# The product with w_out by one level of Strassen's method, in a fused spectral-mixing and squared-ReLU kernel

## The chip, the cores and the metric

The kernel runs on one core of one Trainium2 chip. Times are device microseconds (us) of one execution, and lower is better. Most executions of one kernel agree within 0.3%. An execution that is more than 1.5% above the fastest of the same kernel is called slow and is left out of every comparison.

Engine names are as in the profile: PE is TensorE's matmuls, PEld its weight loads, DVE is VectorE, ACT is ScalarE, POOL is GpSimd.

## The reference

```python
x: (8, 3008, 256) float32;  w_in: (256, 2048) float64;  w_out: (2048, 256) float64
X = fft(fft(x, axis=1), axis=2).real.astype(float32)     # 8 sequences of 3008 rows
h = X.reshape(24064, 256) @ w_in
g = maximum(h, 0) ** 2
out = (g @ w_out).astype(float32)
```

## The kernel before

The transform over the 256 columns is applied to w_in once. The transform over the 3008 rows is made of matrix products, after each sequence's rows have been *folded*: rows that share a table entry are added and subtracted on VectorE. A sequence has six folds and twelve groups of *transform products*. They are made for the next sequence while the main products of the present one run.

The main work is cut into blocks of 256 columns, and a block into 16 *units*, one for each 128 columns of w_in. A unit has a front (two products, then VectorE's combination, then relu and square on ScalarE) and a back (the products with w_out).

```python
def fold(b, t):                                   # six for each sequence
    tt(out=s, in0=v[0::2], in1=v[1::2], op=add)            # fs  } VectorE, two inputs in SBUF each
    tt(out=d, in0=v[0::2], in1=v[1::2], op=subtract)       # fd  }
    # ... load of the next rows ...
    nc.scalar.copy(sc[..., 0:H+1:H], s[..., 0:H+1:H])      # four elements for each partition
    tt(out=sc[..., 1:H], ...); tt(out=dc, ...)
    for kp in range(2):
        tt(out=wP[r, kp], ...); tt(out=wQ[r, kp], ...)
    # ... wE: a copy of one column of wP to all, on ScalarE ...

def front(b, k0, n, fc):
    nc.tensor.matmul(hP, G1[:, fs], pt[:, ks]); nc.tensor.matmul(hQ, G2[:, fs], qt[:, ks])
    nc.vector.scalar_tensor_tensor(out=t, in0=et, scalar=gE[:, fc:fc+1], in1=hP, op0=mult, op1=add)
    tt(out=g[:, 0:n], in0=t, in1=hQ, op=add)               # row k
    tt(out=g[:, n:...][:, ::-1], in0=t, in1=hQ, op=subtract)   # row S - k
    act(g, g, Relu); act(g, g, Square)

def back(b, k0, n, fc, g):
    # for both sides, for each 128 columns of g:
    nc.tensor.matmul(po[s][0:m, j], g[:, ...], wout[:, fc], ...)   # g is the stationary operand
    # after the last fc: copy to SBUF on ScalarE, store

# for each unit: front; back of three units earlier; a share of the next sequence's folds and
# transform products, spread evenly over the sequence
```

A fold's VectorE instructions have both inputs in SBUF, the front's have one in SBUF and one in PSUM, and GpSimd does no arithmetic.

## Time and profile before

The first three executions had a median of 2299.17 us.

| | busy, share of the span | what it does |
|---|---|---|
| TensorE | 96% | two products in the front and four in the back of each unit |
| VectorE | 51% | front, folds, rounding of the float64 weights at the start |
| ScalarE | 46% | relu, square, copies |
| GpSimd | 1% | starts loads, no arithmetic |

This is the groups-of-instructions view of the kernel before, with different shapes kept apart. After the bar come busy us in total and the mean ns of one, then the idle time before it and what ended that.

```profile
L194 DVE TENSOR_TENSOR wP<-sc 128x129 f32<-128x129 f32 x64 | 18.4, 288 | 0.0
L188 DVE TENSOR_TENSOR sc<-fs 128x254 f32<-128x254 f32 x32 | 13.6, 425 | 15.3 <-ACT sc L187 15.3
L189 DVE TENSOR_TENSOR dc<-fd 128x254 f32<-128x254 f32 x32 | 13.4, 417 | 0.0
```

These are the undisturbed lengths: 0.29, 0.43 and 0.42 us. The middle line shows that VectorE waits 15.3/32 = 0.48 us on average for ScalarE's copy of four elements.

### The profile page before, as it was taken

The numbers are of one execution on the slowest core, as the hardware profiler recorded it, in microseconds if no ns is written. First come the engines' busy times: TensorE is split into PE (matmuls) and PEld (weight loads), VectorE is DVE, ScalarE is ACT, GpSimd is POOL, SyncE is SP. The second block draws the span as 40 slices with busy tenths as digits, with TensorE's granted clock in tenths as the row PEclk, the third lists the DMA queues.
The fourth block names the chain that finished last, engine by engine and source line by source line (L and its number), as shares of the span: only waits on it lengthen the run. The fifth ranks groups of instructions, "written<-read, shape, count | busy, mean of one in ns | idle before, by whom it ended". The sixth has DMA issues, their size and how long they took to land.

```text
span 2298.1 us, 26257 instructions
## 1 busy us (share of the span) xinstructions
PE 2213.2 (96%) x9888; PEld 1865.0 (81%) x9888; DVE 1182.4 (51%) x2932; ACT 1049.4 (46%) x1809; POOL 28.1 (1%) x56
## 2 busy tenths in 40 slices
PE   3679999999999999999999999999999999999998
PEld 1357888888888888888888888888888888888887
DVE  5597444654446544474445644465444644444443
ACT  0124444554445444454445544455444544445554
POOL 0000000000000000000000000000000000000000
PEclk7789999999999999999999999999999999999999
DMA  6221000110001000010000100010000000000000
GB/s 212 72 74 45 19 10 10 36 46 10 10 10 54 28 10 10 28 54 10 19 10 27 55 10 10 10 52 30 10 10 18 10 10 10 19 9 10 19 10 18
DMA packets 38528, 64.29 MB, mean 28 GB/s; under 512 B 3448, under 2 KB 27768, under 8 KB 37888
## 3 DMA queue, kind: packets, MB, share of 16 engines
q1 hardware_dynamic: 30096, 33.04, 4.5%
q0 software_dynamic: 7488, 29.31, 4.2%
q8 instruction: 77, 1.26, 0.2%
q14 instruction: 51, 0.42, 0.1%
q10 hardware_dynamic: 816, 0.26, 0.1%
HBM read 37.96 MB, written 24.64 MB: 27 GB/s over the span
## 4 chain that ended last, share of the span: by engine, by line
PE 94%; DVE 5%; ACT 0%; DMA 0%; issue 0%; ACTq 0%; DVEq 0%
PE po L275 57%; PE ph L252 14%; PE ph L251 14%; PE pd L217 8%; PE pg L157 1%; DVE fs L129 0%; DVE fd L134 0%; DVE fs L135 0%; DVE fs L143 0%; DVE fd L133 0%; DVE fs L141 0%; PE pe L162 0%; DVE fs L127 0%; DVE win L144 0%; DVE fd L139 0%; DVE wout L144 0%
## 5 line engine op out<-in xcount | busy, mean ns | idle before, releaser
L275 PE MATMUL po<-wout,g 128*128 128x256 f32 (+1 forms) x6144 | 1460.2, 380 | 1.1 <-ACT g L262 1.1
L275 PEld LDWEIGHTS po<-wout,g 128*128 128x128 f32 (+1 forms) x6144 | 1150.2, 188 | 177.9 <-ACT os L282 6.1
L261 ACT ACTIVATE g<-g 128x512 f32<-128x512 f32 (+2 forms) x768 | 476.2, 620 | 1010.8 <-DVE g L259 983.0
L254 DVE SCALAR_TENSOR_TENSOR he<-Et,gE,ph 128x256 f32<-128x256 f32 (+1 forms) x768 | 364.2, 474 | 859.8 <-PE ph L252 859.2
L262 ACT ACTIVATE g<-g 128x512 f32<-128x512 f32 (+2 forms) x768 | 477.1, 621 | 24.4
L251 PE MATMUL ph<-Pt,G 128*128 128x256 f32 (+1 forms) x1536 | 453.6, 377 | 19.5 <-DVE g L259 19.5
L252 PE MATMUL ph<-Qt,G 127*128 127x256 f32 (+1 forms) x1536 | 453.5, 376 | 0.0
L251 PEld LDWEIGHTS ph<-Pt,G 128*128 128x128 f32 x1536 | 292.8, 191 | 82.3 <-DVE g L259 22.8
L258 DVE TENSOR_TENSOR g<-he,ph 128x256 f32<-128x256 f32 (+1 forms) x768 | 319.5, 416 | 67.3 <-DVE he L254 4.1
L252 PEld LDWEIGHTS ph<-Qt,G 127*128 127x128 f32 x1536 | 294.5, 192 | 33.5
L259 DVE TENSOR_TENSOR g<-he,ph 128x256 f32<-128x256 f32 (+2 forms) x768 | 314.2, 409 | 0.0
L217 PE MATMUL pd<-cosT,wP 128*128 128x377 f32 (+3 forms) x192 | 70.7, 502 | 8.4 <-DVE wP L194 6.0
L217 PE MATMUL pd<-sinT,wQ 128*127 128x377 f32 (+3 forms) x192 | 67.5, 490 | 0.0
L217 PE MATMUL pd<-cosT,wE 128*128 128x377 f32 (+3 forms) x192 | 65.7, 479 | 0.0
L217 PEld LDWEIGHTS pd<-cosT,wP 128*128 128x128 f32 (+1 forms) x192 | 37.0, 197 | 30.7 <-DVE wP L194 8.8
L157 PE MATMUL pg<-win,cosd 128*128 128x512 f32 x16 | 14.9, 1083 | 47.4 <-DVE win L144 47.4
L217 PEld LDWEIGHTS pd<-sinT,wQ 128*127 128x127 f32 (+1 forms) x192 | 37.3, 194 | 20.1 <-issue 1.5
L217 PEld LDWEIGHTS pd<-cosT,wE 128*128 128x128 f32 (+1 forms) x192 | 36.5, 190 | 19.1
L196 ACT COPY wE<-wP 128x256 f32<-128x256 f32 (+2 forms) x48 | 19.4, 403 | 70.0 <-DVE wP L194 70.0
L224 ACT COPY da<-pd 128x377 f32<-128x377 f32 (+3 forms) x48 | 22.7, 473 | 57.3 <-PE pd L217 57.3
L157 PEld LDWEIGHTS pg<-win,cosd 128*128 128x128 f32 x16 | 4.7, 324 | 51.8 <-DVE win L144 26.2
L91 POOL DMA_DIRECT2D xt<-in_x_dram x48 | 25.6, 536 | 1537.8 <-DVE fd L182 1537.0
(38 smaller groups left out, 396.0 us busy)
## 6 DMA issues: line engine op xcount, KB each, us to landing
out_dram<-os SPq DMA_DIRECT2D x72, 256.0 KB
xt<-in_x_dram POOLq DMA_DIRECT2D x32, 512.0 KB, 3.8
raw<-in_moe_w_in_dram SPq DMA_DIRECT2D x8, 512.0 KB
raw<-in_moe_w_out_dram SPq DMA_DIRECT2D x8, 512.0 KB
xt<-in_x_dram POOLq DMA_DIRECT2D x8, 484.0 KB, 4.5
xt<-in_x_dram POOLq DMA_DIRECT2D x8, 480.0 KB, 4.5
out_dram<-os SPq DMA_DIRECT2D x24, 128.0 KB
cosT<-in_cos_s_dram POOLq DMA_DIRECT2D x2, 1131.0 KB, 18.4
```

Of the source, the lines that this page charges most:

```text
L91: nc.gpsimd.dma_start(out=xt[b, t][0:rows], in_=x[b, r0:r0 + rows])
L157: nc.tensor.matmul(ps[0:n], tab[:, i], w[:, i], start=i == 0, stop=i == 1)
L217: nc.tensor.matmul(ps, folded[b, t][which][0:rows, kp, 0:n], tab[0:rows, kp, t, 0:nk], start=i == 0, stop=i == 2)
L224: nc.scalar.copy(st["a"], ps)
L251: nc.tensor.matmul(hP, G1[:, fs], pt[:, ks], start=True, stop=True)
L252: nc.tensor.matmul(hQ, G2[:, fs], qt[:, ks], start=True, stop=True)
L254: nc.vector.scalar_tensor_tensor(out=t, in0=et[:, ks], scalar=gE[:, fc:fc + 1], in1=hP, op0=ALU.mult, op1=ALU.add)
L258: tt(out=g[:, 0:n], in0=t, in1=hQ, op=ALU.add)
L259: tt(out=g[:, n:n + hi - lo][:, ::-1], in0=t[:, lo:hi], in1=hQ[:, lo:hi], op=ALU.subtract)
L261: act(g, g, AF.Relu)
L262: act(g, g, AF.Square)
L275: nc.tensor.matmul(po[s][0:m, j], g[:, g0 + o:g0 + o + m], wout[:, fc], start=fc == 0 and j == 0, stop=fc == NFC - 1, skip_group_check=True)
```

## The change

The intent is to make TensorE's work less. One level of Strassen's method turns a 2 by 2 block product of eight products into one of seven. The price is sums of the operands before and of the results after. The sums of w_out's blocks are made once, those of g in every step, and both go to GpSimd, which was idle. The results now come out transposed, so eight small transposes on TensorE turn each block back. Blocks have 251 columns and six of them cover 1505 rows. A *step* now covers two of the former units.

```diff
+    def combine(n, g):                       # every step, GpSimd
+        gt(out=s1, in0=g21, in1=g22, op=ALU.add)
+        gt(out=s2, in0=s1, in1=g11, op=ALU.subtract)
+        gt(out=s3, in0=g11, in1=g21, op=ALU.subtract)
+        gt(out=s4, in0=g12, in1=s2, op=ALU.subtract)
     def back(n, j, g, s):
-                nc.tensor.matmul(po[s][0:m, j], g[:, ...], wout[:, fc], ...)      # 8 for two units
+        for nm, i, w, v in (("mA", 0, wout[:, 0, j, 0:H], g[:, 0, 0]),             # 7 for a step
+                            ("mA", 1, wout[:, 1, j, 0:H], g[:, 1, 0]),
+                            ("mB", 0, wsum[:, 2, j], g[:, 1, 1]),
+                            ("mB", 1, wout[:, 0, j, H:D], s[:, 0]),
+                            ("mC", 0, wsum[:, 0, j], s[:, 1]),
+                            ("mC", 1, wsum[:, 1, j], s[:, 2]),
+                            ("mD", 0, wout[:, 1, j, H:D], s[:, 3])):
+            nc.tensor.matmul(acc[nm][:, i, 0:n], w, v[:, 0:n], ...)
+    def gather(n):                           # end of a block
+        # mA, mB to SBUF on ScalarE; u2, u3, u4 on VectorE; four sums to c on GpSimd
+    def store(b, k0, n, c):
+        # eight nc.tensor.transpose of c, a copy on ScalarE, store
@@ schedule
-    # folds and transform products of the next sequence spread evenly over its units
+            if b + 1 < B:
+                if at < 9 and at % 3:        # at = step within the sequence, 0 to 47
+                    fold(b + 1, at // 3 * 2 + at % 3 - 1)
+                if at == 10:
+                    dft = dft_ops(b + 1)
+        if at >= 10 and at % NJ == 2:        # NJ = 8 steps for a block
+            for f in dft[:5]:
+                f()
+            dft = dft[5:]
```

Cut: smaller pools, loads of x by another queue, sums of w_out, no wE. The schedule is part of the change. The six folds now stand in the first nine steps of a sequence, and the transform products come five operations at a time.

## The prediction

> **What bounds the kernel now.** I read the page first, engine totals and the chain that ended last:
>
> ```profile
> PE 2213.2 (96%) x9888; PEld 1865.0 (81%) x9888; DVE 1182.4 (51%) x2932; ACT 1049.4 (46%) x1809; POOL 28.1 (1%) x56
> ...
> PE 94%; DVE 5%; ACT 0%; DMA 0%; issue 0%; ACTq 0%; DVEq 0%
> PE po L275 57%; PE ph L252 14%; PE ph L251 14%; PE pd L217 8%; PE pg L157 1%; DVE fs L129 0%; DVE fd L134 0%; DVE fs L135 0%; DVE fs L143 0%; DVE fd L133 0%; DVE fs L141 0%; PE pe L162 0%; DVE fs L127 0%; DVE win L144 0%; DVE fd L139 0%; DVE wout L144 0%
> ```
>
> The chain is TensorE for 94% of the span, 57% of it the product with w_out (po), which the change attacks. VectorE and ScalarE are half idle, GpSimd has nothing to do. Next, whether TensorE has gaps, from busy time by stretches:
>
> ```profile
> 115.00:200.00 85.00, 64.36 (x241) 50.64 (x240) 76.39 (x172) 28.16 (x53) 2.13 (x4) 0.88 0.21 67
> 200.00:2282.00 2082.00, 2082.00 (x9448) 1776.44 (x9447) 1043.46 (x2624) 1005.43 (x1723) 17.03 (x32) 1.00 0.07 20
> ```
>
> The columns after the length are busy us (and instructions) of PE, weight loads, DVE, ACT, POOL, then clock. From 200 us on TensorE is never idle at full clock. Busy is not peak, so I took the rate from the timeline, one unit of a 225-column block:
>
> ```profile
> 402.00 1.89 PE L275 MATMUL po<-wout,g 128*128 128x256 f32 x8
> 402.20 0.45 DVE L254 SCALAR_TENSOR_TENSOR he<-Et,gE,ph 128x225 f32<-128x225 f32 x1 [1.25 <-PE ph L252]
> 402.75 0.39 DVE L258 TENSOR_TENSOR g<-he,ph 128x225 f32<-128x225 f32 x1
> 403.06 0.38 DVE L259 TENSOR_TENSOR g<-he,ph 128x224 f32<-128x224 f32 x1
> ...
> 403.72 0.54 PE L251 MATMUL ph<-Pt,G 128*128 128x225 f32 x2
> 404.10 0.55 PE L252 MATMUL ph<-Qt,G 127*128 127x225 f32 x2
> ...
> 404.49 0.38 PE L275 MATMUL po<-wout,g 128*128 128x256 f32 x1
> ```
>
> Units repeat after 404.49 - 402.00 = 2.49 us for 12 matmul instructions (each product shows as two). In blocks of 256 columns the same view repeats after 2.59 us (131.90 to 134.49), so a 256-column instruction takes 0.216 us and a column about 0.83 ns of it. TensorE streams at its rate and a saved column is a saved time.
>
> **What the Trainium skill says.** "TensorE: Matmul & The Clock Gate", Back-to-back issue gap, gives N/2.4 + 2.5 ns for warm matmuls; "FP8 and Floating Point Precision", TensorE Precision Notes, says true FP32 takes four passes. The trace agrees with both: two instructions of two passes each would be 2 x 256/2.4 + 2.5 = 215.8 ns (estimate from the pages), and 0.216 us is measured. "GPSIMD Engine Reference", Elementwise — side-by-side cycle accounting, gives about 2.6 cycles per element at 1.2 GHz for a two-input FP32 operation. No run yet shows this, since the kernel before has no arithmetic on GpSimd. "SBUF — State Buffer", Who interferes with whom, says that a VectorE instruction with two SBUF inputs and a GpSimd instruction that reads SBUF lock each other out. Not seen here either, for the same reason.
>
> **The change part by part.** *Arithmetic of TensorE, before:* 640 units of 2.59 us and 128 of 2.49 us make 1976 us. The transform products are 96 groups of three, 1.90 us each in the chain in order of time: 182 us. The rest of the span, 2298 - 1976 - 182 = 140 us, is the prologue (main work starts at 115 us, of which 12 groups x 1.9 = 23 us are in the 182, so 92), the stage to about 200 us in which w_out is rounded on VectorE beside the first units (about 39), and the tail (9).
>
> *After:* one step covers two units: four front products and seven for eight, each of 251 columns. An instruction is 215.8 - 5 x 0.83 = 211.7 ns, a step 22 x 211.7 = 4.66 us (4.64 in the block of 250). 8 sequences x 8 steps x 6 blocks give 320 x 4.66 + 64 x 4.64 = 1788 us: 188 us less. Two sources: one product in twelve goes (some 165 us), and w_out's product no longer pads 1505 and 1503 rows to 24 tiles of 128 rows (3072 for 3008).
>
> *Transposes back:* 48 blocks x 8 transposes, each 128 x 126 in and out. The closest row of before is the products of one column, which are limited by weight loads:
>
> ```profile
> 75.76 1.75 PEld L162 LDWEIGHTS pe<-altd,win 128*128 128x128 f32 x15 [0.24 <-issue]
> ```
>
> 15 loads in 1.75 us, 0.117 us each. If a transpose needs one load and one pass (the build marks it as a transpose, so I choose that) a block costs 8 x 0.12 = 1.0 us, 48 us in all; as an ordinary FP32 product of two loads it would be near 95 us.
>
> *VectorE:* the front work is the same (three instructions per half), 1.17 us per half (122.96 - 121.79 at the first units), so 2.34 of 4.66 us. Per block come three sums, about 1.2 us. *ScalarE:* relu and square over 1004 elements; from 579 ns for 449 and 629 ns for 512 elements I get 0.8 ns per element and 1.03 us each, 384 x 2 x 1.03 = 790 us for 953 us before. Copies of two accumulators add 1.2 us per block, the copies for wE go (19 us). Neither bounds. *GpSimd:* 2.6 cycles x 251 / 1.2 GHz = 0.54 us, with start about 0.65 us (estimate from the page): four per step are 2.6 of 4.66 us, 1728 of them 1.12 ms. It has room.
>
> *Latency.* A step's w_out products come two steps after its front, 9.3 us. VectorE ends about 1.5 us after the front, ScalarE at 3.7, GpSimd at 6.4. About three to five us of slack, so steady steps should run without a gap. At a block's end the accumulators have one set of banks: ScalarE copies end 4.3 and 4.9 us after the front, the sums at 5.5; the next block's products want those banks from 4.7 to 7.2 us in the same order, so they just fit. The recombined block c ends at 3.75 + 8 x 0.65 = 9.0 us and its transposes are due at 9.3: tight. I put 15 us for these and for bursts of transform products that wait for ScalarE.
>
> *Fold steps.* This is the largest loss. A fold is 2.68 us of VectorE (80.40 - 77.72 in the timeline), all but nothing of it with two SBUF inputs, now in two steps of every three. In such a step VectorE has 2.34 + 2.68 us; its third instruction waits for a small ScalarE copy (before: 0.46 us on average), which now stands behind relu and square, 2.1 us after the front instead of 0.2: another 1.1 us. That is 6.2 us against 4.66. The six instructions that follow coincide with the four GpSimd sums, and if they lock each other out the step takes up to 8.8 us. Over eight steps with six folds, less 2.5 us that VectorE may lag (two PSUM buffers), that loses 3 to 17 us per sequence, six sequences outside the load stage: 20 to 100 us. I put 35, since the fold's placing looks tuned.
>
> *Load stage.* Rounding 5.15 us + front 2.34 + five folds among eight steps, DMA behind them, GpSimd also forming sums of w_out: about 92 us for 37 us of TensorE work, 55 lost for 39 before. *Tail:* copies, sums, GpSimd, transposes, copy, store: 16 us for 9.
>
> *Sum:* 1788 + 182 + 48 + 92 + 55 + 16 + 35 + 15 = 2231, say 2230 us, 3.0% less.
>
> **The rivals.** (1) VectorE and GpSimd lock each other out in full during folds and in the load stage: +70 to +90 us, about 2310, no gain. For it: the page and the coincidence in time; against: VectorE's lag has room, and only 10 of 26 VectorE instructions in such a step have two SBUF inputs. (2) GpSimd is slower than the estimate. At about 1.05 us per instruction its 36 per block reach the block's 37.3 us plus transposes and it becomes the bound; at 1.2 us the time is 1728 x 1.2 + 200 = 2270 or more, and c comes late at each block. Nothing in the profile of before speaks to it. (3) Transposes as two-pass products: +45 us, 2275. (4) All waits hidden: 1788 + 182 + 48 + 92 + 45 + 14 = 2170.
>
> **Range and chances.** The rivals that lose are one-sided and partly exclusive; 2165 is the floor and 2320 holds one of them in full. Faster by over 2% means under 2253: 0.62; within 2%: 0.30; slower: 0.08.
>
> **What would show it.** TensorE's span of a plain step should be 4.66 us, w_out's products 2688 x 2 instructions and transposes 384 rather than 768; GpSimd near 0.65 us per sum and about half busy; the idle time of TensorE outside the first 200 us under 60 us, released by VectorE's g or he in fold steps. TensorE waiting for GpSimd's s or c in plain steps, or VectorE instructions of the fold lengthened beyond 0.29 to 0.69 us, would make it wrong.

## The result, and the profile after

The changed kernel took 2365.38 us, the median of four runs (2363.64 to 2367.30), against 2299.69 us for the kernel before. The ratio is 1.0287 (95% interval 1.0272 to 1.0302): slower by 2.9%. All ratios in this document are formed from fast runs of the same rounds; they are not quite the ratios of the medians.

The prediction was 2230 us with a range of 2165 to 2320, so the result lies above the range. It gave this outcome a chance of 0.08.

First the page of the changed kernel, engine totals and the chain that ended last:

```profile
PE 2138.7 (90%) x9504; PEld 1788.6 (76%) x9504; DVE 1310.8 (55%) x3076; ACT 920.7 (39%) x1065; POOL 1168.7 (49%) x1776
...
PE 71%; DVE 17%; ACT 7%; POOL 2%; issue 1%; DMA 1%; ACTq 0%; DVEq 0%; SPq 0%; POOLq 0%
PE ph L272 12%; PE ph L273 11%; PE mA L311 11%; PE mB L311 11%; PE mC L311 11%; PE mD L311 6%; PE pd L234 5%; ACT g L280 3%; ACT g L281 3%; DVE g L277 2%; DVE he L275 2%; DVE g L278 2%; PE po L345 2%; DVE wP L210 2%; DVE wQ L211 1%
```

The chain was TensorE for 94% before and is so for 71% now. VectorE has 17% of it, ScalarE 7%. The fold's wP and wQ appear by name. No engine is at its limit by the totals: TensorE is 90% busy for 96% before, VectorE 55% and GpSimd 49%. So look for waits; the next view says where. Busy time by stretches (length, then PE, PEld, DVE, ACT and POOL with instructions, then clock, DMA share and GB/s):

```profile
115.00:200.00 85.00, 41.86 (x135) 32.62 (x134) 75.56 (x143) 14.64 (x18) 30.92 (x52) 0.74 0.19 62
...
800.00:1100.00 300.00, 282.81 (x1274) 238.62 (x1273) 164.03 (x390) 121.45 (x140) 150.58 (x227) 0.98 0.08 23
...
2000.00:2100.00 100.00, 99.50 (x471) 86.44 (x470) 50.02 (x128) 47.28 (x53) 58.19 (x90) 1.00 0.04 11
```

From 2000 to 2100 us there are no folds, and after 2015 us no transform products either, and TensorE is idle for 0.5 us. From 800 to 1100 us it is idle for 17.2 us of 300, where before it had no idle time at all after 200 us. What ended TensorE's waits (us in total, times, longest):

```profile
PE ph L272 <- DVE g L278: 104.9, 38, 8.4
PE pg L167 <- DVE win L154: 47.4, 4, 15.4
PE pd L234 <- ACT da L241: 35.4, 14, 3.9
PE mC L311 <- DVE u L326: 14.8, 6, 2.5
```

The second line is the prologue, and it was the same before. The first was 19.5 us in 7 waits before: the front's products cannot start because VectorE has not read the last front. The third are transform products waiting for a ScalarE copy, and the fourth are main products waiting for VectorE's sums at a block's end.

The waits are not the whole price. This is the stretch without start and tail, by the same view:

```profile
240.00:2355.00 2115.00, 2005.88 (x9090) 1701.13 (x9088) 1147.44 (x2747) 884.57 (x1010) 1111.43 (x1679) 0.98 0.07 20
```

TensorE is idle for 2115.00 - 2005.88 = 109 us of it, and its granted clock (the share of TensorE's full speed, as the trace records it) is 0.98, where the kernel before had 1.00 after 200 us. The trace's clock records show 22 stretches at half clock, 81.9 us together, or 41 us of work at full clock. Of these, 20 began within 2 us of the end of a TensorE wait of 2.1 to 3.0 us; not every such wait was followed by one. It shows in the products: two instructions of the front took 1.14 us at 1064.62, in such a stretch, and 0.59 us at 1082.87, after it.

The undisturbed steps do what was wanted. TensorE's timeline in the last sequence:

```profile
2209.73 1.04 PE L345 MATMUL po<-ident,c 128*126 128x128 f32 x8
2210.60 1.01 PE L311 MATMUL mA<-g,wout 128*128 128x251 f32 x4
...
2215.28 1.01 PE L311 MATMUL mA<-g,wout 128*128 128x251 f32 x4
```

A step repeats after 2215.28 - 2210.60 = 4.68 us, where 4.66 was predicted, and eight transposes take 2210.60 - 2209.73 = 0.87 us of TensorE. A plain block of eight steps and its transposes takes 38.3 us. Here is the fold in its step, from the timeline of an earlier sequence:

```profile
1016.43 0.69 DVE L199 TENSOR_TENSOR fd<-xt 128x512 f32<-128x512 f32 x1
...
1018.03 0.18 ACT L204 COPY sc<-fs 128x4 f32<-128x4 f32 x1
1018.20 0.63 POOL L291 TENSOR_TENSOR s<-g 128x251 f32<-128x251 f32 x1 [2.98 <-ACT sc L204]
1018.24 0.87 DVE L205 TENSOR_TENSOR sc<-fs 128x254 f32<-128x254 f32 x1 [1.12 <-ACT sc L204]
...
1018.91 0.78 POOL L292 TENSOR_TENSOR s<-s,g 128x251 f32<-128x251 f32 x1
1019.03 0.93 DVE L206 TENSOR_TENSOR dc<-fd 128x254 f32<-128x254 f32 x1
...
1019.64 0.90 POOL L293 TENSOR_TENSOR s<-g 128x251 f32<-128x251 f32 x1
1019.88 0.80 DVE L210 TENSOR_TENSOR wP<-sc 128x129 f32<-128x129 f32 x1
...
1020.50 0.68 POOL L294 TENSOR_TENSOR s<-g,s 128x251 f32<-128x251 f32 x1
1020.61 0.71 DVE L211 TENSOR_TENSOR wQ<-dc 128x127 f32<-128x127 f32 x1
1021.25 0.28 DVE L210 TENSOR_TENSOR wP<-sc 128x129 f32<-128x129 f32 x1
```

Read the start times of the two engines against each other: they take turns, one instruction each. The wP at 1019.88 starts while a GpSimd sum runs (1019.64 to 1020.54) and ends 0.14 us after it, 0.80 us in all. The wP at 1021.25, after the last sum, takes 0.28 us. (As 0.28 is more than 0.14, the records of the two still overlap by a part; that one engine is shut out for the whole of the other's instruction is not shown.) The copy of four elements also matters. It stands behind relu and square on ScalarE and ends at 1018.21, just when square has released GpSimd's first sum. The copy does not only cost VectorE 1.12 us: it holds the fold back until the sums begin, and so lines the two up.

Over the whole run, the groups with shapes kept apart:

```profile
L345 PE MATMUL po<-ident,c 128*126 128x128 f32 x320 | 41.5, 272 | 0.0
L210 DVE TENSOR_TENSOR wP<-sc 128x129 f32<-128x129 f32 x64 | 37.5, 587 | 0.0
L206 DVE TENSOR_TENSOR dc<-fd 128x254 f32<-128x254 f32 x32 | 27.4, 857 | 0.0
L205 DVE TENSOR_TENSOR sc<-fs 128x254 f32<-128x254 f32 x32 | 24.9, 777 | 25.9 <-ACT sc L204 25.9
```

The mean wP went from 288 to 587 ns, dc from 417 to 857, sc from 425 to 777. wQ went from 285 to 476, fs from 685 to 768 and fd from 685 to 782. With two wP and two wQ, a fold grew by 2 x 299 + 2 x 191 + 440 + 352 + 83 + 97 = 1952 ns, 1.95 us, and the wait for the copy from 0.48 to 25.9/32 = 0.81 us.

The transform products wait in another place. The timeline of the step at a block's end where five operations come at once:

```profile
1066.39 4.51 PE L234 MATMUL pd<-cosT,wP 128*128 128x377 f32 x12
...
1070.91 1.04 ACT L280 ACTIVATE g<-g 128x1004 f32<-128x1004 f32 x1 [3.23 <-DVE g L278]
...
1072.92 0.46 ACT L241 COPY da<-pd 128x377 f32<-128x377 f32 x1
...
1073.43 5.76 PE L234 MATMUL pd<-sinT,wQ 128*127 128x377 f32 x12 [2.53 <-ACT da L241]
```

TensorE filled both buffers of such products and stands for 2.53 us until ScalarE copies one out. ScalarE does relu and square of the step first, and those began late because VectorE did the block's three sums ahead of that step's front. The twelve instructions after the wait take 5.76 us where two groups at full clock take 2 x 1.90 = 3.80: a stretch at half clock began at 1074.3.

To put sizes on these I took the time from one block's first sum on VectorE to the next one's. In a steady sequence the six blocks take 53.4, 50.0, 51.9, 44.8, 38.3 and 41.8 us, 280.2 in all. Without a wait it would be 6 x 38.3 + 12 x 1.90 = 252.6. Taking off each block's own transform products leaves a loss of 18.6 us for folds and 8.9 us for the bursts. The other sequences are much the same (18.6 to 20.1 and 7.3 to 9.0); over all of them folds lose 117 us and bursts 55, of which idle time and half clock (109 + 41 us) make up most. The whole is then: products and transposes 1836, transform 182, prologue 92, load stage loss 69 (the first block's sums begin at 226.46, and by my estimate 42.3 us after the first front at 115.37 would be possible), folds 117, bursts 55, tail 12. That makes 2363 us of the 2365.

### The profile page after: what moved, and what is told of

The parts are those of the page before. It is cut to its first block, busy times and chain, and to the rows that moved or that the text cites. A ratio compares the mean times of both kernels' runs of the same rounds, so it can differ in the third digit from the quotient of the medians.

```text
span 2365.2 us, 26858 instructions
## 1 busy us (share of the span) xinstructions
PE 2138.7 (90%) x9504; PEld 1788.6 (76%) x9504; DVE 1310.8 (55%) x3076; ACT 920.7 (39%) x1065; POOL 1168.7 (49%) x1776
## 3 DMA queue, kind: packets, MB, share of 16 engines
q8 instruction: 74, 1.21, 0.2%
## 4 chain that ended last, share of the span: by engine, by line
PE 71%; DVE 17%; ACT 7%; POOL 2%; issue 1%; DMA 1%; ACTq 0%; DVEq 0%; SPq 0%; POOLq 0%
PE ph L272 12%; PE ph L273 11%; PE mA L311 11%; PE mB L311 11%; PE mC L311 11%; PE mD L311 6%; PE pd L234 5%; ACT g L280 3%; ACT g L281 3%; DVE g L277 2%; DVE he L275 2%; DVE g L278 2%; PE po L345 2%; DVE wP L210 2%; DVE wQ L211 1%
## 5 line engine op out<-in xcount | busy, mean ns | idle before, releaser
L280 ACT ACTIVATE g<-g 128x1004 f32<-128x1004 f32 (+1 forms) x384 | 399.2, 1040 | 1246.2 <-DVE g L278 845.7
L291 POOL TENSOR_TENSOR s<-g 128x251 f32<-128x251 f32 (+1 forms) x384 | 243.0, 633 | 1001.1 <-ACT g L281 913.7
L275 DVE SCALAR_TENSOR_TENSOR he<-Et,gE,ph 128x251 f32<-128x251 f32 (+1 forms) x768 | 362.5, 472 | 656.3 <-PE ph L273 656.0
L272 PE MATMUL ph<-Pt,G 128*128 128x251 f32 (+1 forms) x1536 | 472.5, 389 | 106.2 <-DVE g L278 104.9
L273 PE MATMUL ph<-Qt,G 127*128 127x251 f32 (+1 forms) x1536 | 466.1, 385 | 0.0
L311 PE MATMUL mC<-s,wsum 128*128 128x251 f32 (+1 forms) x1536 | 392.7, 377 | 14.8 <-DVE u L326 14.8
L281 ACT ACTIVATE g<-g 128x1004 f32<-128x1004 f32 (+1 forms) x384 | 399.1, 1039 | 12.1
L311 PE MATMUL mA<-g,wout 128*128 128x251 f32 (+1 forms) x1536 | 393.5, 378 | 0.0
L277 DVE TENSOR_TENSOR g<-he,ph 128x251 f32<-128x251 f32 (+1 forms) x768 | 320.5, 417 | 57.3 <-POOL s L293 0.5
L311 PEld LDWEIGHTS mC<-s,wsum 128*128 128x128 f32 x1536 | 292.4, 191 | 52.6 <-issue 17.0
L311 PEld LDWEIGHTS mA<-g,wout 128*128 128x128 f32 x1536 | 288.6, 192 | 44.0 <-ACT sA L321 4.1
L278 DVE TENSOR_TENSOR g<-he,ph 128x251 f32<-128x251 f32 (+1 forms) x768 | 314.1, 409 | 0.0
L293 POOL TENSOR_TENSOR s<-g 128x251 f32<-128x251 f32 (+1 forms) x384 | 287.9, 750 | 0.0
```

Of the source, the lines that this page charges most:

```text
L272: nc.tensor.matmul(hP, G1[:, fs], pt[:, ks], start=True, stop=True)
L273: nc.tensor.matmul(hQ, G2[:, fs], qt[:, ks], start=True, stop=True)
L275: nc.vector.scalar_tensor_tensor(out=t, in0=et[:, ks], scalar=gE[:, fc:fc + 1], in1=hP, op0=ALU.mult, op1=ALU.add)
L277: tt(out=g[:, h, 0, 0:n], in0=t, in1=hQ, op=ALU.add)
L278: tt(out=g[:, h, 1, 0:n][:, ::-1], in0=t, in1=hQ, op=ALU.subtract)
L280: act(v, v, AF.Relu)
```

## The experiments

Twelve kernels were run, in three calls of four, each on another chip. The kernel before had medians of 2298.69, 2299.77 and 2299.58 us. Each kernel ran four times. All results were correct except that of e3_no_reads.

The theory is that the fold's VectorE instructions and GpSimd's sums exclude each other, and that the bursts add a second loss. The rivals are that VectorE simply has too much to do in these steps, that the ScalarE copy alone is the cost, or that the shorter back gives the pipeline less slack.

### e1_spread: the transform products one operation in every second step

```diff
-        if at >= 10 and at % NJ == 2:
-            for f in dft[:5]:
+        if at >= 10 and at % 2 == 0:
+            for f in dft[:1]:
```

> The only edit: the 13 transform operations of the next sequence are issued one every second step instead of five in one step. My theory: in a burst the third and fourth group of products wait for ScalarE's copy of the first, which stands behind relu and square, and this costs about 9 us per sequence (block times 50.0 and 51.9 us against 45.9 and 47.8 of pure work), seven times, so 2365 should fall to 2300 to 2315 us and the fold stretches stay as they are. Rival: what is lost there is VectorE work that only moves elsewhere; then the time stays within 10 us of 2365.

Measured: 2320.42 us, the median of the three fast runs, ratio to before 1.0092 (1.0075 to 1.0109), some 45 us below the changed kernel. One execution, the profiled one, was slow (5681.44 us). So this won 45 of the 55 us that the block times put down to the bursts. The time is a little over what I expected.

### e2_copy_on_dve: the copy of four elements on VectorE

```diff
-        nc.scalar.copy(sc[r, :, 0:H + 1:H], s[r, :, 0:H + 1:H])
+        nc.vector.tensor_copy(sc[r, :, 0:H + 1:H], s[r, :, 0:H + 1:H])
```

> The only edit: the four-element copy inside a fold is done by VectorE instead of ScalarE, so that the fold need not wait behind relu and square. Theory: a fold then takes 2.7 us on VectorE right after the front work and is nearly over when the GpSimd sums begin, so both the 1.1 us wait and most of the lengthening by the shared lock (1.9 us per fold) go; of the 18.6 us lost to folds per sequence 12 to 18 come back, 70 to 110 us in all: 2255 to 2295 us. Rival (GpSimd's lock does not depend on that order, or the loss is the sheer VectorE work): at most 25 us, 2340 or more.

Measured: 2306.98 us, ratio 1.0035 (1.0020 to 1.0050), 58 us less than the changed kernel. The loss for folds went from 18.6 to 10.1 us in a sequence. So the wait behind relu and square matters, but the fold still meets the sums. The result lies between what the theory and the rival expected.

### e3_no_reads: GpSimd writes without reading

```diff
-        gt(out=s1, in0=g21, in1=g22, op=ALU.add)
-        gt(out=s2, in0=s1, in1=g11, op=ALU.subtract)
-        gt(out=s3, in0=g11, in1=g21, op=ALU.subtract)
-        gt(out=s4, in0=g12, in1=s2, op=ALU.subtract)
+        for v in (s1, s2, s3, s4):
+            nc.gpsimd.memset(v, 1.0)
```

> Wrong result on purpose: the four GpSimd sums of a step are replaced by four fills of the same outputs, which read nothing. The wait for ScalarE's copy stays. If the lock between two-input VectorE instructions and reading GpSimd instructions lengthens the fold (theory), the fold's instructions go back to 0.29 to 0.69 us as in the kernel before, the fold loss falls from 18.6 to some 5 us per sequence and the load stage gains up to 15 us: 2260 to 2300 us. If only the wait for ScalarE matters (rival), fold instructions stay near 0.8 us or the time stays above 2340.

Measured: 2278.36 us, ratio 0.9908 (0.9892 to 0.9925), 87 us less than the changed kernel. The groups of this run:

```profile
L210 DVE TENSOR_TENSOR wP<-sc 128x129 f32<-128x129 f32 x64 | 21.5, 337 | 0.0
L206 DVE TENSOR_TENSOR dc<-fd 128x254 f32<-128x254 f32 x32 | 13.4, 418 | 0.0
```

VectorE has the same instructions at the same places, and their lengths are those of before again (dc 418 for 417; wP 337 for 288, because six of all 96 wP met a sum at a block's end, which still reads, and took 0.81 us). The fold's loss falls from 18.6 to 5.9 us in a sequence. The fills are also shorter (0.31 us) than the sums, and the products' operands come sooner, so the 87 us are an upper mark for the exclusion by itself. The lengths are the direct evidence.

### e4_spread_copy: both legal edits together

The edits of e1_spread and e2_copy_on_dve.

> Edits of the two others together, right result. Theory: both losses are separate and add: 2365 - 55 - 90 = 2220, range 2190 to 2250 us, which beats the kernel before (2299) by 2 to 5 per cent. Rival (the transform products, spread out, collide with the folds or the stores and give the gain back): 2260 or more.

Measured: 2253.59 us, the median of three fast runs, ratio 0.9804 (0.9788 to 0.9820). That is 112 us less than the changed kernel, a little more than 45 and 58 together. So the two gains add. By the interval it stays unclear whether this is 2% faster than the kernel before. It missed my range at the top. One execution, again the profiled one, was slow (6773.93 us).

### e5_paced: no two folds in neighbouring steps

```diff
-                if at < 9 and at % 3:
-                    fold(b + 1, at // 3 * 2 + at % 3 - 1)
-                if at == 10:
+                f0 = 2
+                if f0 <= at < f0 + 12 and at % 2 == 0:
+                    fold(b + 1, (at - f0) // 2)
+                if at == f0 + 12:
                     dft = dft_ops(b + 1)
```

On top of e4_spread_copy. The idea was that a step without a fold gives VectorE time to recover.

> The spread transform and the copy on VectorE as before, and in addition the six folds stand in every second step (steps 2, 4 to 12 of a sequence) instead of in two of every three. Theory: a fold step takes 5.2 us of VectorE against 4.66 us of TensorE, so after two in a row VectorE is late and meets the GpSimd sums again; with a plain step between, it catches up. The fold loss should fall from about 10 to 0 to 4 us per sequence, 2254 to 2195 to 2220 us. Rival (any fold beside the sums costs its locked time whatever the spacing): 2240 us or more.

Measured: 2284.86 us, ratio 0.9937 (0.9922 to 0.9952). My reason for this one fell: it is 31 us slower than e4_spread_copy. The timeline shows what happens at one such place:

```profile
1255.63 0.63 POOL L291 TENSOR_TENSOR s<-g 128x251 f32<-128x251 f32 x1 [5.24 <-ACT g L281]
...
1256.73 1.21 DVE L199 TENSOR_TENSOR fd<-xt 128x512 f32<-128x512 f32 x1
...
1258.48 0.62 POOL L294 TENSOR_TENSOR s<-g,s 128x251 f32<-128x251 f32 x1
...
1259.07 0.80 POOL L291 TENSOR_TENSOR s<-g 128x251 f32<-128x251 f32 x1
...
1263.73 0.69 PE L272 MATMUL ph<-Pt,G 128*128 128x251 f32 x2 [1.56 <-DVE g L278]
```

A late step brings the sums of two steps back to back on GpSimd (the second four start at 1259.07, when the first four have just ended), and they lie under the next fold from its first instruction to its last but one (fd takes 1.21 us for 0.69). The folds lose 15.4 us in a sequence, for 10.1 in e2_copy_on_dve with the folds in pairs. So a whole fold after the front collided in both placings, and taking folds out of neighbouring steps did not help.

### e6_paced_late: the first sequence's folds after w_out is rounded

```diff
-                f0 = 2
+                f0 = 2 if b else 8
```

> As the last, and for the first sequence the folds of the second stand at steps 8 to 18, after w_out is rounded, not among the rounding. Theory: the load stage loses 68 us because rounding, folds and DMA of raw words behind the loads of x share VectorE and one queue; without folds there it is rounding 5.2 + front 2.3 us per step, 60 us for 37 of TensorE work, so 25 to 45 us less than e5: 2160 to 2190 us. Rival (the rounding's own lock with GpSimd is what costs): at most 10 us less than e5.

Measured: 2281.56 us, ratio 0.9921, only 3 us less than e5_paced. That meets the rival's mark, but not its reason: the first block's sums began at 204.6 us for 219.0, so 14 us were won in the load stage, and the later folds gave 11 of them back.

### e7_eight and e8_eight_only: eight products and no sums

Both replace the seven products by the eight of before in the new layout, and drop all sums. e7_eight does this to e6_paced_late, e8_eight_only to the changed kernel itself.

```diff
-            flight.append((b, k0, n, j, g, combine(n, g)))
+            flight.append((b, k0, n, j, g))
     # back: for h in 0, 1; for c in 0, 1; for i in 0, 1:
+                    nc.tensor.matmul(acc[nm][:, i, 0:n], wout[:, c, j, h * H:(h + 1) * H], g[:, c, i, 0:n], ...)
     # gather: two copies on ScalarE, no sums
```

> e6 with the ordinary eight products in place of seven and no sums on GpSimd or VectorE (right result, same blocks, same transposes). Theory: the saved product is worth its own TensorE time once the schedule hides the rest, 384 x 0.423 = 162 us: 150 to 170 us more than e6, about 2330. Rival (the sums cost as much as the product saves): within 60 us of e6.

> The changed kernel's own schedule (bursts, folds in two of three steps, copy on ScalarE) with eight products and no sums. Theory: 162 us of products more, and 70 to 100 us of lock fewer (as in the run with fills, and more time per step for VectorE): 2390 to 2460 us. Rival (the loss in the fold stretches is VectorE's and ScalarE's order alone, not GpSimd's sums): 2490 us or more.

Measured: e7_eight 2314.62 us (ratio 1.0066), 33 us more than e6_paced_late. e8_eight_only 2352.46 us (ratio 1.0231, 1.0215 to 1.0246), which is 13 us *less* than the changed kernel. Both came out below what I expected, and e7_eight at its rival's mark (within 60 us). The reason shows only with e12_split_eight, below.

e8_eight_only is the plainest verdict on the change. Eight products for seven are 384 steps x 2 x 0.2117 us = 163 us more of TensorE, and yet the version with the extra product is faster. Its steady sequence takes 274.5 us where 6 x 41.7 + 22.8 = 273.0 would be without a wait. Folds and bursts, which stand in the same steps as in the changed kernel, lose 1.5 us in a sequence for 27.5. So the places of folds and bursts and the wait for the copy do not make the loss by themselves: in that run VectorE waits for the copy just as it does with e3_no_reads, 31.0 us for the 32 folds of full height. This run alone does not separate GpSimd's sums from two other things, since the longer step also gives VectorE 3.4 us per block more room, and the three sums at a block's end are gone. For the fold e3_no_reads does, which has the short step and VectorE's full work.

### e9_split: each fold cut in two, each half in a step of its own

```diff
-                if at < 9 and at % 3:
-                    fold(b + 1, at // 3 * 2 + at % 3 - 1)
-                if at == 10:
+                f0 = 2 if b else 8
+                if f0 <= at < f0 + 12:
+                    if at % 2 == 0:
+                        half = fold(b + 1, (at - f0) // 2)        # fs, fd
+                    else:
+                        fold2(b + 1, (at - f0) // 2, *half)       # copy on VectorE, sc, dc, wP, wQ
+                if at == f0 + 12:
```

On top of e6_paced_late, from which only the cut differs (the diff is against the changed kernel). GpSimd's four sums take about 2.7 us of a 4.66 us step, which leaves some 1.9 us between those of one step and of the next. The front does not mind the sums; a fold of 2.7 us does not fit the gap, but half of one about does.

> The spacing run fell: a fold in every second step lost 15 us per sequence instead of 10. New theory, from its trace: after a late step VectorE hands over two steps' work in quick succession, ScalarE and GpSimd follow one step behind, and the eight sums run just under the next fold. What counts is that a fold is short enough to fit in the 2.3 us between the end of the front work and the start of GpSimd's sums. Here a fold is cut in two: its first two instructions (1.37 us) in one step, the other seven (1.8 us) in the next, so VectorE has at most 4.2 of 4.66 us and nothing meets. Theory: fold loss 0 to 2 us per sequence, no lengthened instruction, 2170 to 2205 us. Rival (a fold costs its lock wherever it stands): 2250 or more.

Measured: **2175.42 us**, ratio 0.9459 (0.9444 to 0.9475). This beats the kernel before by 5.4% and the changed kernel by 8%. One such step in its timeline:

```profile
1729.88 0.71 POOL L298 TENSOR_TENSOR s<-g 128x251 f32<-128x251 f32 x1
...
1730.40 0.41 DVE L283 TENSOR_TENSOR g<-he,ph 128x251 f32<-128x251 f32 x1
1730.55 0.62 POOL L299 TENSOR_TENSOR s<-g,s 128x251 f32<-128x251 f32 x1
1730.72 0.48 DVE L209 COPY sc<-fs 128x4 f32<-128x4 f32 x1
...
1731.91 0.29 DVE L215 TENSOR_TENSOR wP<-sc 128x129 f32<-128x129 f32 x1
...
1733.09 0.63 POOL L296 TENSOR_TENSOR s<-g 128x251 f32<-128x251 f32 x1 [1.92 <-ACT g L286]
```

The front (L283, one input in PSUM) runs under a sum and keeps its 0.41 us. The sums end at 1731.17 and the next begin at 1733.09, and the fold's second half lies between them, with wP at 0.29 us. In the first half fs is still lengthened (1071 ns on average for 685), because it meets the end of the sums, but the slack takes it; so my "no lengthened instruction" missed. From 260 us to the last sequence's end TensorE is idle for only 5.2 us, at a clock of 1.00:

```profile
260.00:2165.00 1905.00, 1899.79 (x8851) 1640.10 (x8849) 1070.31 (x2717) 854.63 (x948) 1068.49 (x1636) 1.00 0.07 22
```

A steady sequence takes 253.5 us against the 252.6 that are possible. The instructions are those of the changed kernel, 9504 on TensorE in both, and VectorE has the copies besides. So too much work for VectorE, or too short a step, is not the cause by itself: both are here, without the loss.

### e10_split_copy_act, e11_split_burst, e12_split_eight: one part of e9_split undone at a time

The first puts the copy of four elements back on ScalarE, the second puts the transform products back into bursts of five, the third has eight products and no sums.

```diff
 # e10_split_copy_act, in the second half of the fold
-        nc.vector.tensor_copy(sc[r, :, 0:H + 1:H], s[r, :, 0:H + 1:H])
+        nc.scalar.copy(sc[r, :, 0:H + 1:H], s[r, :, 0:H + 1:H])
 # e11_split_burst
-        if at >= 10 and at % 2 == 0:
-            for f in dft[:1]:
+        if at >= 10 and at % NJ == 2:
+            for f in dft[:5]:
```

> e9 with the four-element copy back on ScalarE, where it stands behind relu and square of the second half's step. Theory: the second half then begins 2.3 us late, just with the sums, and is lengthened by the lock; VectorE has 2.3 + 2.3 + 3 us in that step: 20 to 70 us more than e9. Rival (the copy's place does not matter once the fold is cut): within 10 us of e9.

> e9 with the transform products again in bursts of five operations. Theory: the bursts cost the same 8 to 9 us per sequence as in the changed kernel, 45 to 65 us more than e9. Rival (that loss came only with the folds): within 15 us of e9.

> e9 with eight products and no sums. Theory: in this schedule the saved product is worth nearly its full 162 us: 110 to 160 us more than e9, about 2310. Rival (the sums eat most of it): within 60 us of e9.

Measured against e9_split of the same rounds:

| | us | ratio to before | more than e9_split |
|---|---|---|---|
| e9_split | 2175.42 | 0.9459 (0.9444 to 0.9475) | |
| e10_split_copy_act | 2285.27 | 0.9936 (0.9921 to 0.9951) | 110 |
| e11_split_burst | 2219.10 | 0.9653 (0.9639 to 0.9668) | 44 |
| e12_split_eight | 2315.07 | 1.0070 (1.0055 to 1.0085) | 140 |

e10_split_copy_act costs more than I expected, and the groups say why:

```profile
L215 DVE TENSOR_TENSOR wP<-sc 128x129 f32<-128x129 f32 x64 | 36.8, 575 | 0.0
...
L210 DVE TENSOR_TENSOR sc<-fs 128x254 f32<-128x254 f32 x32 | 25.9, 811 | 65.5 <-ACT sc L209 65.5
```

VectorE waits 65.5/32 = 2.05 us for the copy, and by then the sums have begun: wP is at 575 ns again. An instruction of 0.18 us on ScalarE, standing behind relu and square, costs 110 us by moving six others under the sums. The bursts cost 44 us here, just under my range, and 45 in e1_spread. e12_split_eight says what the saved product is worth once the sums stand clear of the folds: 140 of its 163 us.

With e6_paced_late and e7_eight it also makes a table of two by two:

| | seven products, with sums | eight products, no sums |
|---|---|---|
| whole folds | e6_paced_late 2281.56 | e7_eight 2314.62 |
| cut folds | e9_split 2175.42 | e12_split_eight 2315.07 |

Cutting the folds is worth 106 us beside the sums and nothing without them. A steady sequence of e7_eight takes 273.0 us, which is the time without a wait, although its folds are whole.

## Why the prediction was wrong

**The arithmetic of TensorE was right** where nothing waits. A step took 4.68 us for the predicted 4.66. (In "TensorE: Matmul & The Clock Gate", Back-to-back issue gap, the formula that the prediction used is given for isolated matmuls; that it fits this stream is what the trace shows.) The transposes need one load and one pass, 384 of each as predicted, at 0.87 us for eight where 1.0 was put, and the 182 us of transform products and 92 us of prologue stood. Rival (3), two-pass transposes, is out.

**GpSimd was right.** The sums took 0.63 to 0.75 us on average for the predicted 0.65, and GpSimd was 49% busy. Rival (2) is out. The latency step held for plain steps and for block ends in the last sequence, which run without a gap; elsewhere main products waited six times for the sums at a block's end, 14.8 us.

**The fold step failed**, and with it the prediction. The text found the mechanism and put bounds on it, 3 to 17 us per sequence and 20 to 100 in all, and then wrote: "I put 35, since the fold's placing looks tuned". It measured 18.6 to 20.1 us per sequence and 117 in all, above even the upper bound. The choice of 35 rested on no view of the profile. Rival (1) had the mechanism right, and its "against" was wrong in two ways. It counted that only 10 of 26 VectorE instructions in such a step have two SBUF inputs. By the kernel it is 8 of 14, the whole fold, and six of them stand together, held back by a copy behind the same relu and square that release the four sums. And it trusted in VectorE's lag of 2.5 us, which did not hide the loss. The wait for the copy was priced there as 1.1 us of delay; e10_split_copy_act shows that its real price is the alignment with the sums. And no term of the sum holds the half clock after TensorE's waits.

The prediction's own signs said so too: the fold's instructions were lengthened to as much as 0.93 us, past the 0.29 to 0.69 us that it allowed, and TensorE was idle for 2082.00 - 1965.16 = 117 us between 200 and 2282 us, where under 60 was forecast.

**"15 us for these and for bursts" was mis-sized.** The bursts lost 55 us by the block times, and taking them away won 45 and 44 us in two runs. I had the copies of the accumulators in view, and not that a third group of products needs a buffer that ScalarE empties only after a late relu and square.

**The load stage** lost 69 us for the predicted 55; the tail 12 for 16.

With 117 for 35, 55 for 15, 69 for 55 and 12 for 16 the predicted 2231 becomes 2363, of the measured 2365. Rival (1) said about 2310 and fell short mainly by the bursts. Rival (4), all waits hidden, said 2170. That was not the changed kernel but turned out to be e9_split, at 2175 (its load stage lost 43 us for the rival's 45): the arithmetic of the change was worth what it promised, and its schedule was not fit for it.

What stays open: how the loss of a fold divides between idle time and half clock, and why only some waits were followed by half clock. The slow executions of e1_spread and e4_spread_copy are also unexplained.

## What to carry to other kernels

Work that goes to an idle engine must be priced by the instructions of its neighbours that it will coincide with, and not by the busy shares: 55% and 49% here hid a loss of over 100 us. When two engines exclude each other, find the gap in one engine's work within a step, and cut the other's side work to fit it; that was worth far more here than spreading it out. And look at what releases the two sides: a tiny instruction on a third engine can line them up.

## What the Trainium skill lacked or had wrong

- "SBUF — State Buffer", Who interferes with whom, was right on who contends: with reading sums wP took 587 ns, with fills that only write 337, and the front with one SBUF input kept its 0.41 us under a sum. Its general rule calls the shared ports "an exclusive lock", and that the other engine "fully blocks" for the whole instruction it says of the two-port modes. For two-input instructions against GpSimd's reads it gives no price. Here a wP of 0.28 us took 0.80, and GpSimd's sums rose from 0.72 to 0.90; the wP ended 0.14 us after the sum that it met.
- "GPSIMD Engine Reference", Elementwise — side-by-side cycle accounting, gives 2.6 cycles per element, 0.54 us for 251 elements at 1.2 GHz. The trace has 0.63 or 0.72 us for sums alone, which leaves 0.09 to 0.18 us for start and end. The page names dispatch and completion as such terms, but gives no total for short instructions.
- "TensorE: Matmul & The Clock Gate", Part 4: PE-mode transpose, gives 275 to 390 ns for a bf16 transpose of 128 by 128. For FP32 of 128 by 126 the page has no rate of issue: here eight in a row took 0.87 us, 0.11 us each, with one load and one matmul instruction for each, while the recorded length of 272 ns is close to its lower figure.
- No page that I read describes whole executions as slow as these: 5681 and 6774 us, one in four runs of two kernels that otherwise took 2320 and 2254 us, with TensorE shown as 99% busy at a clock of 1.00. A plain block took 105 us in both, and 145 in the first half of the second, for 38.3 in fast runs.
